# A fused attention, mixture and gated feed-forward kernel: splits, sums and changeover operands moved to neighbouring units, first-layer weights loaded mid-products, the last attention block's normalisation issued first

## The chip, the cores and the metric

The kernel runs on one core of one Trainium2 chip. The metric is the device time of one execution in microseconds (us); the median of three executions of the kernel before is 633.32 us, from 632.99 to 634.52. A measurement of this kernel tells a difference of about 0.3% from none.

The engines are TensorE (PE; PEld is its weight load), VectorE (DVE), ScalarE (ACT), GpSimd (POOL) and SyncE (SP), which issues all transfers.

## The reference, cut to what matters

Three parts run one after the other. All inputs and the output are float32; w_in and w_out reach the chip as 64-bit words.

```python
# q, k, v: (2, 8, 576, 64); a window of 64 keys
scores = q @ k.T / 8, masked to 0 <= row - col < 64
x = softmax(scores) @ v                       # as (1152, 512)

# moe: 4 experts, w1 (4, 512, 1024), w2 (4, 1024, 512)
p = domain_probs / domain_probs.sum(-1)
x = sum over e of p[:, e] * (relu(x @ w1[e]) @ w2[e])

# moe2: w_in (512, 2048), w_out (2048, 512), alpha (2048)
h = x @ w_in
out = (max(h, 0) + alpha * min(h, 0)) @ w_out
```

## The kernel before, in words

Every operand of a product is split into a high and a low part (ACT rounds the high part, `split` at L215, and VectorE or GpSimd subtracts it, `low` at L211), and each product is three matmuls: low by high, high by low, high by high. In names, `wfh`/`wfl` are the first-layer weights, `w2h`/`w2l` the second-layer ones, `xah`/`xal` and `xth`/`xtl` the x operands, `hh`/`hl` the hidden layer.

The 1152 tokens are two halves, p = 0 with 512 and p = 1 with 640. The hidden columns are twelve stages s of 512: stages 0 to 7 are the four experts (two stages each), 8 to 11 (`S1` = 8, `NST` = 12) the second layer pair. Stage 0 runs in chunks of tokens beside the attention (units `LC` and `BC`, four chunks). From stage 1 on a stage is:

- `A` units, seven for each half: the first layer's 2 x 2 block product done as seven products (`PRODUCTS`, L414) with sums of blocks as operands, for two column halves u. Three PSUM banks X, Z and W of each u take several products in turn. `product` (L418) issues the matmuls, copies a bank away on ACT (`keep`, L435), adds it back on VectorE (`total`, L440) and hands the finished quarter to `evict` (L472). A later product adds on to a bank only when the copy or the total has read it.
- `B` units, one for each 128 tokens (four for p = 0, five for p = 1): the second layer (`l2_unit`, L549), 12 matmuls of 512 columns each, added to `acc` by VectorE (ACT in stage 8).

In stages 8 to 11 `evict` only makes r on ACT; `activate` (L518) makes the gated value on VectorE (a head), then its high part on ACT and its low part on GpSimd (a tail); its second argument says how many tails are left waiting. Stage 8 has the order A of half 0, B of half 0 (tokens 2, 3, 0, 1), A of half 1, B of half 1, because its x is the output of stage 7: `x2_unit` (L575) transposes it on TensorE, seven times within stage 7's end and twice within stage 8's first products.

The engines are in order, and the order is written by hand. The list `order` (L682 to L689) holds the units. Every other step hangs on a unit through `plan` (L695): it is issued right behind that unit's own instructions. So hang the sums of first-layer weight blocks (`w_sums`, L174, four GpSimd operations into one buffer `sr` that the next sums can take when its split is done), the splits of first-layer weights (`w_split`, L189) and second-layer weights (`split_w2`, L232), and at the changeover the x operands (`x_first`, `x_sum`, `x_split`, list `changes` at L726). The subtraction on VectorE that ends a split is held until the next unit (`pending`, `settle` at L205).

Weight tiles (`ws`, two buffers of 1 MB) are loaded when the tile two before was last used (`loads`, L768 to L771); SP issues them in the same order of units. The 64-bit words of w_in and w_out are turned to float32 on the chip (`conv_steps`, L251) in steps of three phases, a word tile each three steps: ACT reads the words (L279, L280) and GpSimd ends the tile before (L292, L293); VectorE (L282, L283) and a store; VectorE (L286) and the load of the tile after next. `pace` (L779) says how many of these steps a unit takes.

The attention goes in 18 blocks j of 64 tokens with steps S (scores), E (exponentials), N (normalise: two small VectorE operations, one GpSimd multiply, L330), PT (transposes), PV (product with v) and, five times, X (an x operand of half 0: `x_second`, L395). L605 to L634 write their order; a chunk's units take a share of the list by count, behind each unit.

Of the kernel before, what the change touches and what calls it, by code (L numbers as in the profile page):

```python
# [26 lines left out]
def tile_kernel(ctx, tc, q, k, v, probs, w1, w2, w_in, w_out, alpha, out):  # L27
    nc = tc.nc


    B, H, D, S = k.shape
# [11 lines left out]
    NBLK = B * NB  # L43
    S1 = E * F // FS
    SPE = F // FS
    NST = S1 + F2 // FS
# [19 lines left out]
    def psum(name):  # L66
        return pp.tile([P, 512], F32, tag="ps", name=name)
# [27 lines left out]
    for c in range(1, NCH):  # L95
        n = CHUNK[c + 1] - CHUNK[c]
# [68 lines left out]
    A11, A12, A22, SA1, SA2, SA3, SA4 = range(7)  # L165
# [252 lines left out]
    def product(s, p, u, i):  # L418
        n = HALF[p]
        st = sets.setdefault((s, p, u), {})  # L420
        wi, (kind, f), bank = PRODUCTS[i]
        first = bank not in st
        if first:
            st[bank] = psum(f"{bank}{s}_{p}_{u}")[:, 0:n]
        ps = st[bank]
        wh, wl = [x[:, wi] for x in wf_t[s, u]]
        xh, xl = [x[:, f:f + 2] for x in xa[p]] if kind == "a" else [x[:, f] for x in xt[p]]
        m = 0
        for w, x in ((wl, xh), (wh, xl), (wh, xh)):
            for d in range(2):  # L430
                nc.tensor.matmul(ps, lhsT=w[:, d, :], rhs=x[:, d, :], start=(first and m == 0), stop=(m == 5),  # L431
                                 skip_group_check=True)
                m += 1

        def keep(name):  # L435
            t = late["wfp"].tile([P, HALF[1]], F32, tag=name, bufs=2, name=f"{name}{s}_{p}_{u}")[:, 0:n]
            st[name] = t
            nc.scalar.activation(out=t, in_=ps, func=AF.Copy)  # L438

        def total(name):  # L440
            t = st[name]
            nc.vector.tensor_tensor(out=t, in0=ps, in1=t, op=ALU.add)  # L442
            return t

        if i == 0:
            keep("s1")
        elif i == 1:
            keep("z1")
        elif i == 2:
            keep("u2")  # L450
        elif i == 3:
            evict(s, p, 2 * u, 0, total("s1"))
        elif i == 4:
            evict(s, p, 2 * u + 1, 1, total("z1"))
        elif i == 5:
            evict(s, p, 2 * u, 1, total("u2"))
        else:
            evict(s, p, 2 * u + 1, 0, ps, True)
            del sets[s, p, u]
        if s >= S1:  # L460
            activate(1 if i > 2 else 0, int(i < 5) if s == S1 else (2, 0, 4)[min(i, 2)])
        else:
            low_parts(1)

# [21 lines left out]
    def low_parts(keep):  # L486
        while len(lows) > keep:
            hl, src, hh = lows.pop(0)
            nc.vector.scalar_tensor_tensor(out=hl, in0=src, scalar=0.0, in1=hh.bitcast(F32),
                                           op0=ALU.max, op1=ALU.subtract)  # L490
# [27 lines left out]
    def activate(keep, later):  # L518
        while len(heads) > keep:
            hh, hl, r, col, src, g = heads.pop(0)  # L520
            nc.vector.scalar_tensor_tensor(out=g, in0=r, scalar=col, in1=src, op0=ALU.mult, op1=ALU.add)
            tails.append((hh, hl, g))
        while len(tails) > later:
            hh, hl, g = tails.pop(0)
            nc.scalar.activation(out=hh, in_=g, func=AF.Copy)  # L525
            nc.gpsimd.tensor_tensor(out=hl, in0=g, in1=hh.bitcast(F32), op=ALU.subtract)  # L526
# [54 lines left out]
    with tc.manual_schedule():  # L581
# [22 lines left out]
        steps = []  # L604
        for j in range(NBLK + 4):  # L605
            last = (j - 3) * BLK in CHUNK[1:]
            pv = [("PV", j - 4)] if 0 <= j - 4 < NBLK else []

            if last:
                steps += pv  # L610
            apart = 6 <= j - 1 < 14
            if apart:
                steps.append(("E", j - 1))
            if 0 <= j - 3 < NBLK:
                steps.append(("PT", j - 3))
            if 3 < j <= NBLK and not apart:
                steps.append(("N", j - 1))
            if j < NBLK:
                steps.append(("S", j))
                if not 6 <= j < 14:  # L620
                    steps.append(("E", j))
            if 0 < j <= 3:
                steps.append(("N", j - 1))
            if not last:
                steps += pv
            if apart:
                steps.append(("N", j - 1))
            if 2 <= j < 2 + NF:
                steps.append(("W", j - 2))
            if j % GB == 0 and 3 <= j // GB + 2 < NG:  # L630
                steps.append(("Q", j // GB + 2))

            if 13 <= j < 18:
                steps.append(("X", j - 13))  # L634
        pos = [0]

        def att_step():
# [52 lines left out]
        at = {u: n for n, u in enumerate(order)}  # L690
# [4 lines left out]
        def plan(unit, fn, tid, *args):  # L695
            work.setdefault(at[unit], []).append((fn, tid, args))
# [3 lines left out]
        for s in range(1, NST):  # L700
            if s == 1:
                lc, b = [[(k, NCH - 1, t) for t in range(3)] for k in ("LC", "BC")]
                for u in range(2):
                    plan(lc[u], w_sums, (1, s), s, u, nc.gpsimd)
                for u, part, unit in ((0, A11, ("X1",)), (1, A11, b[0]), (0, SA1, b[0]), (1, SA1, b[1]),
                                      (0, A22, b[2]), (1, A22, b[2])):
                    plan(unit, w_split, (1, s), s, u, part)
            else:
                b = [("B", s - 1, x, t) for x in range(2) for t in range(NTT[x])]
                if s == S1 + 1:  # L710
                    b = [("B", S1, 1, t) for t in (3, 3, 4, 4, 0, 1)]
                plan(("A", s - 1, 1, 0 if s > S1 else 2), w_sums, (1, s), s, 0, nc.gpsimd)
                plan(b[2], w_sums, (1, s), s, 1, nc.gpsimd)
                for n, part in ((0, A11), (0, A22), (1, SA1)):
                    plan(b[n], w_split, (1, s), s, 0, part)
                for n, part in ((2, A11), (3, A22), (4, SA1)):
                    plan(b[n], w_split, (1, s), s, 1, part)
            units = [(0, 1), (0, 2), (1, 0), (1, 1)]
            if s in (1, S1):
                units = [(int(s == 1), i) for i in (0, 0, 1, 1)]  # L720
            for f, (p, i) in enumerate(units):
                plan(("A", s, p, i), split_w2, (2, s), s, f)

        half = {p: [(0, HALF[p] // 2), (HALF[p] // 2, HALF[p] // 2)] for p in range(2)}
        first, second = half[0]
        changes = [(("B", S1 - 1, 0, 3), 0, (0,), (), first), (("B", S1 - 1, 1, 0), 0, (0,), (), second),  # L726
                   (("B", S1 - 1, 1, 0), 0, (), (1, 2, 3, 4), first), (("B", S1 - 1, 1, 1), 0, (), (1, 2, 3, 4), second),
                   (("B", S1 - 1, 1, 1), 0, (1, 2), (), first), (("B", S1 - 1, 1, 2), 0, (1, 2), (), second),
                   (("B", S1 - 1, 1, 2), 0, (3, 5), (), first), (("B", S1 - 1, 1, 3), 0, (3, 5), (), second),
                   (("B", S1 - 1, 1, 4), 0, (4,), (), first), (("B", S1 - 1, 1, 4), 0, (4,), (), second)]  # L730
        for o in half[1]:
            changes += [(("A", S1, 0, 2), 1, (), (1,), o), (("A", S1, 0, 3), 1, (), (2,), o),
                        (("B", S1, 0, 2), 1, (0, 1), (), o), (("B", S1, 0, 3), 1, (2,), (3,), o),
                        (("B", S1, 0, 0), 1, (3, 5), (4,), o), (("B", S1, 0, 1), 1, (4,), (), o)]
        for unit, p, splits, sums, (o, w) in changes:
            for f in splits:
                if f == 0:
# [22 lines left out]
        uses = {}  # L760
# [4 lines left out]
        tids = sorted(uses, key=lambda x: uses[x][0])  # L765
        tids = [(1, 0)] + tids
        uses[1, 0] = [-1]
        loads = {}  # L768
        for n, tid in enumerate(tids):
            if n >= 2:  # L770
                loads.setdefault(uses[tids[n - 2]][-1] + (tids[n - 2][1] > 0), []).append(tid)  # L771

        marks = [steps.index(("PV", CHUNK[c + 1] // BLK - 1)) + 1 for c in range(NCH)]
        per = [len(LC(c) + BC(c)) for c in range(NCH)]
# [3 lines left out]
            load_w(tid)  # L778
        def pace(op, s=0, p=0, i=0):  # L779
            if op == "A":  # L780
                return int(2 <= s < S1 and i < 2 + (s == S1 - 1) or S1 < s < NST - 1 and i in (1, 2))
            if op != "B" or s in (S1 - 1, NST - 2, NST - 1) or (s, p) == (S1, 0):
                return 0
            return 1

        pend = []
        for i, unit in enumerate(order):
            op = unit[0]
# [35 lines left out]
            for _ in range(pace(*unit)):  # L824
                next(late["steps"], None)
# [4 lines left out]
            if op in ("LC", "BC") and unit[1] < NCH - 1:  # L830
                c = unit[1]
                n = (unit[2] if op == "LC" else NF + unit[2]) + 1
# [41 lines left out]
```

## Time and profile before

| | |
|---|---|
| runs of before, median (lowest to highest) | 633.32 us (632.99 to 634.52) |
| the profiled execution's own time | 634.3 us |
| its span, first to last instruction | 632.5 us |
| busy share of the span: TensorE, weight load | 97%, 87% |
| busy share: VectorE, ScalarE, GpSimd | 73%, 50%, 45% |
| mean granted TensorE clock | 0.992 |
| chain that ended last, TensorE's share | 83% |

Times in rows are microseconds from the start of the span, then the duration; `x2` after an operation counts instructions merged into one row. In brackets stands the idle time of the engine before the row and what released it. PEclk is the TensorE clock granted, 1.00 being the full 2.4 GHz and 0.50 the level of 1.2 GHz. A matmul row's duration is longer than its share of the pipeline, so the distance of two starts tells more.

### The profile page before, as it was taken

The numbers are of one execution on the slowest core, as the hardware profiler recorded it, in microseconds if no ns is written. First come the engines' busy times: TensorE is split into PE (matmuls) and PEld (weight loads), VectorE is DVE, ScalarE is ACT, GpSimd is POOL, SyncE is SP. The second block draws the span as 40 slices with busy tenths as digits, with TensorE's granted clock in tenths as the row PEclk, the third lists the DMA queues.
The fourth block names the chain that finished last, engine by engine and source line by source line (L and its number), as shares of the span: only waits on it lengthen the run. The fifth ranks groups of instructions, "written<-read, shape, count | busy, mean of one in ns | idle before, by whom it ended". The sixth has DMA issues, their size and how long they took to land.

```text
span 632.5 us, 10897 instructions
## 1 busy us (share of the span) xinstructions
PE 612.8 (97%) x4032; PEld 548.9 (87%) x4032; DVE 462.6 (73%) x933; ACT 315.7 (50%) x789; POOL 285.4 (45%) x301
## 2 busy tenths in 40 slices
PE   4899999999999999999999999999999999999998
PEld 3688789989989988989989988989788978988986
DVE  3766649778789788788789788757867789763642
ACT  5756526633724624624724624636766662751730
POOL 5645651143443466053443463614735676661440
PEclk8899989999999999999999999999999999999999
DMA  9842001415316225324316224012302124110012
GB/s 323 310 153 68 2 1 64 138 33 183 118 46 205 84 84 183 100 68 167 118 54 196 84 83 150 18 35 98 135 1 108 59 103 136 34 63 1 2 50 101
DMA packets 31653, 62.60 MB, mean 99 GB/s; under 512 B 2288, under 2 KB 11760, under 8 KB 30576
## 3 DMA queue, kind: packets, MB, share of 16 engines
q1 hardware_dynamic: 31600, 61.90, 29.0%
q8 instruction: 32, 0.52, 0.3%
q14 instruction: 21, 0.17, 0.1%
HBM read 51.14 MB, written 10.75 MB: 98 GB/s over the span
## 4 chain that ended last, share of the span: by engine, by line
PE 83%; DVE 5%; ACT 4%; DMA 2%; POOL 2%; issue 2%; SPq 0%; ACTq 0%; POOLq 0%; DVEq 0%
PE o L545 40%; PE X L431 19%; PE Z L431 9%; PE W L431 4%; PE oc L533 4%; PE h L500 3%; ACT p L327 1%; DMA ws<-in_moe_w_dram 1%; PE pv L357 1%; DMA wd<-in_moe_w_in_dram 1%; POOL hl L526 1%; PE s L309 1%; DVE w2l L212 1%; PE pt L340 1%; ACT w2h L219 1%
## 5 line engine op out<-in xcount | busy, mean ns | idle before, releaser
L545 PE MATMUL o<-w2h,hl 128*128 128x512 f32 (+1 forms) x400 | 155.7, 389 | 0.6 <-POOL hl L526 0.5
L545 PE MATMUL o<-w2l,hh 128*128 128x512 f32 (+1 forms) x400 | 155.6, 389 | 0.4 <-ACT hh L525 0.4
L545 PE MATMUL o<-w2h,hh 128*128 128x512 f32 (+1 forms) x400 | 154.9, 387 | 0.0
L292 POOL TENSOR_TENSOR ct<-ct 128x512 f32<-128x512 f32 x32 | 42.7, 1335 | 133.3 <-DVE ct L291 58.1
L545 PEld LDWEIGHTS o<-w2h,hl 128*128 128x128 f32 x400 | 75.1, 188 | 18.3 <-POOL hl L526 3.2
L545 PEld LDWEIGHTS o<-w2l,hh 128*128 128x128 f32 x400 | 75.2, 188 | 15.0 <-ACT hh L525 0.6
L545 PEld LDWEIGHTS o<-w2h,hh 128*128 128x128 f32 x400 | 75.2, 188 | 14.9
L564 DVE SCALAR_TENSOR_TENSOR acc<-o,pn,acc 128x512 f32<-128x512 f32 x63 | 47.1, 748 | 40.7 <-PE o L545 40.6
L187 POOL TENSOR_TENSOR sr<-ws 128x256 f32<-128x256 f32 x44 | 41.6, 944 | 58.9 <-DVE wfl L212 53.0
L212 DVE SCALAR_TENSOR_TENSOR w2l<-ws,w2h 128x512 fp32r<-128x512 f32 x48 | 43.8, 918 | 25.6 <-ACT w2h L219 25.2
L431 PE MATMUL X<-xth,wfl 128*128 128x256 f32 (+1 forms) x264 | 57.4, 298 | 2.8 <-DVE z L442 1.7
L431 PE MATMUL X<-xtl,wfh 128*128 128x256 f32 (+1 forms) x264 | 56.6, 296 | 0.0
L431 PE MATMUL X<-xth,wfh 128*128 128x256 f32 (+1 forms) x264 | 56.6, 296 | 0.0
L293 POOL TENSOR_TENSOR ct<-ct 128x512 f32<-128x512 f32 x32 | 48.3, 1508 | 2.5
L280 ACT ACTIVATE ct<-wd 128x512 f32<-128x512 f32 x32 | 21.3, 665 | 50.8 <-DVE ct L286 50.8
L219 ACT ACTIVATE wfh<-sr 128x1024 fp32r<-128x1024 f32 x22 | 23.1, 1056 | 45.8 <-POOL sr L187 45.8
L431 PEld LDWEIGHTS X<-xth,wfl 128*128 128x128 f32 x264 | 42.5, 190 | 3.8 <-DVE z L442 2.3
L431 PEld LDWEIGHTS X<-xth,wfh 128*128 128x128 f32 x264 | 42.7, 190 | 0.0
L431 PEld LDWEIGHTS X<-xtl,wfh 128*128 128x128 f32 x264 | 42.6, 190 | 0.0
L568 DVE TENSOR_TENSOR acc<-o,acc 128x512 f32<-128x512 f32 (+1 forms) x28 | 18.7, 668 | 29.7 <-PE o L545 29.7
L526 POOL TENSOR_TENSOR hl<-s,hh 128x256 fp32r<-128x256 f32 (+1 forms) x16 | 13.4, 860 | 56.7 <-ACT hh L525 56.7
L438 ACT ACTIVATE s<-X 128x256 f32<-128x256 f32 (+1 forms) x44 | 18.0, 411 | 40.1 <-PE X L431 40.0
(157 smaller groups left out, 1440.5 us busy)
## 6 DMA issues: line engine op xcount, KB each, us to landing
ws<-in_moe_w_dram SPq DMA_DIRECT2D x16, 1024.0 KB, 5.9
wd<-in_moe_w_in_dram SPq DMA_DIRECT2D x16, 512.0 KB, 3.8
cv<-ct SPq DMA_DIRECT2D x32, 256.0 KB, 3.0
wd<-in_moe_w_out_dram SPq DMA_DIRECT2D x16, 512.0 KB, 3.7
ws<-cv SPq DMA_DIRECT2D x8, 1024.0 KB, 5.2
v<-in_v_dram SPq DMA_DIRECT2D x16, 256.0 KB, 5.4
q<-in_q_dram SPq DMA_DIRECT2D x6, 384.0 KB, 6.7
out_dram<-acc SPq DMA_DIRECT2D x8, 256.0 KB, 2.0
```

Of the source, the lines that this page charges most:

```text
L187: e.tensor_tensor(out=t4[:, o], in0=x, in1=y, op=op)
L212: nc.vector.scalar_tensor_tensor(out=lv, in0=src, scalar=1.0, in1=hv.bitcast(F32), op0=ALU.mult, op1=ALU.subtract)
L219: nc.scalar.activation(out=hv, in_=src, func=AF.Copy)
L280: nc.scalar.activation(out=a, in_=top.bitcast(F32), func=AF.Abs, scale=LIFT)
L292: nc.gpsimd.tensor_tensor(out=y, in0=y, in1=e, op=ALU.mult)
L293: nc.gpsimd.tensor_tensor(out=y, in0=r, in1=y, op=ALU.add)
L431: nc.tensor.matmul(ps, lhsT=w[:, d, :], rhs=x[:, d, :], start=(first and m == 0), stop=(m == 5), skip_group_check=True)
L500: nc.tensor.matmul(ps, lhsT=w[:, d * P:(d + 1) * P], rhs=x[:, d, :], start=(m == 0), stop=(m == 3 * KD - 1))
L526: nc.gpsimd.tensor_tensor(out=hl, in0=g, in1=hh.bitcast(F32), op=ALU.subtract)
L533: nc.tensor.matmul(ps, lhsT=h_c[c, f][a][:, t * P:(t + 1) * P], rhs=w_t[2, 0, f][b], start=(n == 0), stop=(n == 3 * NF - 1))
L545: nc.tensor.matmul(ps, lhsT=h_t[s, p, f][a][:, t * P:(t + 1) * P], rhs=w_t[2, s, f][b][:, cols], start=(n == 0), stop=(n == 3 * NF - 1))
L564: nc.vector.scalar_tensor_tensor(out=at, in0=ps, scalar=sc, in1=at, op0=ALU.mult, op1=ALU.add)
```

## The change

In order of the diff: in stage 8 no tail is left waiting. In the attention the normalisation of the last block (j = 17) goes ahead of the transposes of block 15, and each X step is issued one block earlier. For stages 10 and 11 the sums of first-layer weights move from the A units of the stage before into its B units (u = 0 from the first product of half 1 to B unit 1, u = 1 from B unit 2 to B unit 4), and the splits of these sums two units later. Second-layer weights are split at the products 0 and 1 of half 0 in place of 1 and 2. For stage 8's half 1 the first two differences of x move from the A units (GpSimd) to B unit 2 (VectorE), and the splits and sums behind them one unit later each. First-layer weights of stage 2 and later are loaded not before product 3 of half 0 of the stage before. The conversion steps move: stage 7's third step of each half goes, stage 1's B units 1 and 3 take two, stages 9 and 10 take them at the products 0 and 1, and B unit 0 of half 0 takes none from stage 9 on. The name `late_sums` is not used.

```diff
--- before.py
+++ after.py
@@ -458,7 +458,7 @@
             evict(s, p, 2 * u + 1, 0, ps, True)
             del sets[s, p, u]
         if s >= S1:
-            activate(1 if i > 2 else 0, int(i < 5) if s == S1 else (2, 0, 4)[min(i, 2)])
+            activate(1 if i > 2 else 0, 0 if s == S1 else (2, 0, 4)[min(i, 2)])
         else:
             low_parts(1)
 
@@ -611,9 +611,11 @@
             apart = 6 <= j - 1 < 14
             if apart:
                 steps.append(("E", j - 1))
+            if j == NBLK:
+                steps.append(("N", j - 1))
             if 0 <= j - 3 < NBLK:
                 steps.append(("PT", j - 3))
-            if 3 < j <= NBLK and not apart:
+            if 3 < j < NBLK and not apart:
                 steps.append(("N", j - 1))
             if j < NBLK:
                 steps.append(("S", j))
@@ -630,8 +632,8 @@
             if j % GB == 0 and 3 <= j // GB + 2 < NG:
                 steps.append(("Q", j // GB + 2))
 
-            if 13 <= j < 18:
-                steps.append(("X", j - 13))
+            if 12 <= j < 17:
+                steps.append(("X", j - 12))
         pos = [0]
 
         def att_step():
@@ -709,13 +711,15 @@
                 b = [("B", s - 1, x, t) for x in range(2) for t in range(NTT[x])]
                 if s == S1 + 1:
                     b = [("B", S1, 1, t) for t in (3, 3, 4, 4, 0, 1)]
-                plan(("A", s - 1, 1, 0 if s > S1 else 2), w_sums, (1, s), s, 0, nc.gpsimd)
-                plan(b[2], w_sums, (1, s), s, 1, nc.gpsimd)
-                for n, part in ((0, A11), (0, A22), (1, SA1)):
+                late_sums = s > S1 + 1
+                behind = 2 * (s > S1 + 1)
+                plan(b[1] if behind else ("A", s - 1, 1, 0 if s > S1 else 2), w_sums, (1, s), s, 0, nc.gpsimd)
+                for n, part in ((0, A11), (0, A22), (1 + behind, SA1)):
                     plan(b[n], w_split, (1, s), s, 0, part)
-                for n, part in ((2, A11), (3, A22), (4, SA1)):
+                plan(b[2 + behind], w_sums, (1, s), s, 1, nc.gpsimd)
+                for n, part in ((2, A11), (3, A22), (4 + behind, SA1)):
                     plan(b[n], w_split, (1, s), s, 1, part)
-            units = [(0, 1), (0, 2), (1, 0), (1, 1)]
+            units = [(0, 0), (0, 1), (1, 0), (1, 1)]
             if s in (1, S1):
                 units = [(int(s == 1), i) for i in (0, 0, 1, 1)]
             for f, (p, i) in enumerate(units):
@@ -729,9 +733,11 @@
                    (("B", S1 - 1, 1, 2), 0, (3, 5), (), first), (("B", S1 - 1, 1, 3), 0, (3, 5), (), second),
                    (("B", S1 - 1, 1, 4), 0, (4,), (), first), (("B", S1 - 1, 1, 4), 0, (4,), (), second)]
         for o in half[1]:
-            changes += [(("A", S1, 0, 2), 1, (), (1,), o), (("A", S1, 0, 3), 1, (), (2,), o),
-                        (("B", S1, 0, 2), 1, (0, 1), (), o), (("B", S1, 0, 3), 1, (2,), (3,), o),
-                        (("B", S1, 0, 0), 1, (3, 5), (4,), o), (("B", S1, 0, 1), 1, (4,), (), o)]
+            changes += [(("B", S1, 0, 2), 1, (0,), (1,), o), (("B", S1, 0, 3), 1, (1,), (), o),
+                        (("B", S1, 0, 0), 1, (2, 5), (3,), o), (("B", S1, 0, 1), 1, (3,), (), o),
+                        (("A", S1, 1, 0), 1, (4,), (), o)]
+        for unit, f in ((("B", S1, 0, 2), 2), (("B", S1, 0, 1), 4)):
+            changes += [(unit, 1, (), (f,), o) for o in half[1]]
         for unit, p, splits, sums, (o, w) in changes:
             for f in splits:
                 if f == 0:
@@ -768,7 +774,10 @@
         loads = {}
         for n, tid in enumerate(tids):
             if n >= 2:
-                loads.setdefault(uses[tids[n - 2]][-1] + (tids[n - 2][1] > 0), []).append(tid)
+                free = uses[tids[n - 2]][-1] + (tids[n - 2][1] > 0)
+                if tid[0] == 1 and tid[1] > 1:
+                    free = max(free, at["A", tid[1] - 1, 0, 3])
+                loads.setdefault(free, []).append(tid)
 
         marks = [steps.index(("PV", CHUNK[c + 1] // BLK - 1)) + 1 for c in range(NCH)]
         per = [len(LC(c) + BC(c)) for c in range(NCH)]
@@ -778,10 +787,10 @@
             load_w(tid)
         def pace(op, s=0, p=0, i=0):
             if op == "A":
-                return int(2 <= s < S1 and i < 2 + (s == S1 - 1) or S1 < s < NST - 1 and i in (1, 2))
-            if op != "B" or s in (S1 - 1, NST - 2, NST - 1) or (s, p) == (S1, 0):
+                return int(2 <= s < S1 and i < 2 or S1 < s < NST - 1 and i < 2)
+            if op != "B" or s in (S1 - 1, NST - 2, NST - 1) or (s, p) == (S1, 0) or s > S1 and (p, i) == (0, 0):
                 return 0
-            return 1
+            return 1 + (s == 1 and p == 0 and i % 2)
 
         pend = []
         for i, unit in enumerate(order):
```

## Rows read from the trace of the kernel before

**Rows 1.** The page, busy time by engine: us (share of the span) xinstructions.

```profile
PE 612.8 (97%) x4032; PEld 548.9 (87%) x4032; DVE 462.6 (73%) x933; ACT 315.7 (50%) x789; POOL 285.4 (45%) x301
```

**Rows 2.** The chain of waits, TensorE's pieces: start us, us, what.

```profile
196.16 1.43 PE X L431 x12
...
243.06 1.43 PE X L431 x12
...
290.65 1.43 PE X L431 x12
...
416.93 2.78 PE o L545 x12
420.14 2.76 PE o L545 x12
...
436.13 1.44 PE X L431 x12
...
486.64 1.43 PE X L431 x12
...
510.99 24.51 PE o L545 x108
535.50 1.43 PE X L431 x12
```

**Rows 3.** The timeline of TensorE, rows with idle time before them.

```profile
79.51 0.66 PE L340 MATMUL pt<-ident,p 128*128 128x128 f32 x4 [1.79 <-POOL p L334]
...
251.97 0.50 PE L431 MATMUL X<-xth,wfl 128*128 128x256 f32 x2 [0.28 <-DVE z L442]
...
391.31 0.50 PE L431 MATMUL X<-xth,wfl 128*128 128x256 f32 x2 [1.12 <-ACT u L438]
...
448.66 0.50 PE L545 MATMUL o<-w2h,hl 128*128 128x512 f32 x1 [0.46 <-POOL hl L526]
...
495.67 0.50 PE L431 MATMUL X<-xth,wfl 128*128 128x256 f32 x2 [0.40 <-DVE z L442]
...
508.90 0.56 PE L431 MATMUL X<-xth,wfl 128*128 128x320 f32 x2 [0.97 <-DVE z L442]
```

**Rows 4.** Busy us by stretch: PE, PEld, DVE, ACT, POOL, then PEclk, DMA, GB/s.

```profile
80.00:84.00 4.00, 4.00 (x40) 3.41 (x39) 1.87 (x4) 0.38 (x1) 3.76 (x7) 0.57 0.02 4
...
391.00:392.00 1.00, 0.69 (x5) 0.69 (x6) 0.94 (x3) 1.00 (x3) 0.31 (x1) 1.00 0.00 0
```

**Rows 5.** The timeline of GpSimd.

```profile
77.19 1.27 POOL L401 TENSOR_TENSOR xtl<-tr,xth 128x512 fp32r<-128x512 f32 x1
78.42 1.04 POOL L334 TENSOR_TENSOR p<-p,st 128x512 f32<-128x512 f32 x1
...
441.64 2.60 POOL L389 TENSOR_TENSOR tr<-raw,tr 128x320 f32<-128x320 f32 x2
445.98 1.76 POOL L526 TENSOR_TENSOR hl<-s,hh 128x256 fp32r<-128x256 f32 x2 [1.73 <-ACT hh L525]
...
506.22 1.19 POOL L187 TENSOR_TENSOR sr<-ws,sr 128x256 f32<-128x256 f32 x1
...
524.11 1.13 POOL L187 TENSOR_TENSOR sr<-ws 128x256 f32<-128x256 f32 x1 [1.16 <-DVE wfl L212]
```

**Rows 6.** The timeline of VectorE.

```profile
250.35 1.22 DVE L212 SCALAR_TENSOR_TENSOR w2l<-ws,w2h 128x512 fp32r<-128x512 f32 x1
...
441.27 2.23 DVE L212 SCALAR_TENSOR_TENSOR w2l<-ws,w2h 128x512 fp32r<-128x512 f32 x2 [0.52 <-ACT w2h L219]
...
452.73 0.92 DVE L212 SCALAR_TENSOR_TENSOR xal<-raw,xah 128x640 fp32r<-128x640 f32 x1 [2.60 <-ACT xah L219]
...
542.02 0.68 DVE L212 SCALAR_TENSOR_TENSOR w2l<-ws,w2h 128x512 fp32r<-128x512 f32 x1
```

**Rows 7.** The timeline of ScalarE, a conversion step of stage 7.

```profile
389.77 0.67 ACT L279 ACTIVATE ct<-wd 128x512 f32<-128x512 uint32 x1 [1.45 <-DMA wd<-in_moe_w_in_dram]
```

**Rows 8.** The page, transfers: what, queue, count, KB each, median us to landing.

```profile
ws<-in_moe_w_dram SPq DMA_DIRECT2D x16, 1024.0 KB, 5.9
```

## The prediction

> **What bounds the kernel now.** I read the page first, for the engine that is full. TensorE is busy for 612.8 of 632.5 us [rows 1], so at most 19.7 us can come back unless work is taken off TensorE, and the change takes none off: every product stays.
>
> Then I read the chain of waits for where the stages begin. A stage s is seven product steps for each half of the tokens (the A units) and nine output units (the B units). Stage 3 runs from 196.16 to 243.06, which is 46.90 us, and the whole stage is TensorE work [rows 2]. That is the yardstick. Stage 4 takes 47.59, so 0.69 is lost. Stages 5 to 7 together take 145.48, which is 4.78 over three times 46.90. Seven sets of transposes lie in stage 7; each lengthens an output unit from 2.72 (24.51 / 9) to 3.21, 0.49 each, 3.4 in all, and the other 1.4 us are lost. Stage 8 takes 50.51: less 46.90 and two more sets of transposes, 2.6 are lost. Stage 9 takes 48.86, so 1.96 are lost. Together 6.6 us.
>
> Third, TensorE's timeline tells where these losses sit and who released them [rows 3]. The first of them, at 79.51, belongs to the attention: 1.79 us of waiting for GpSimd's multiply of the last block's probabilities. Behind it the granted clock is 0.57 of full speed over the 4 us from 80 to 84 [rows 4], which costs 4 x 0.43 = 1.7 us more. At 251.97, 495.67 and 508.90 the seventh product of a set waits: it adds to the bank X, which VectorE's total behind the fifth has to read first. The wait at 391.31 is the same kind, on ScalarE's copy of the third. The one at 448.66 is an output unit that waits for the low half of its operand from GpSimd.
>
> So there is 1.8 + 1.7 + 0.7 + 1.4 + 2.6 + 2.0 = 10.2 us that a better order could give back, and the start (before 24 us) is not touched.
>
> **The change part by part.**
>
> *Attention.* GpSimd's last multiply (1.04 us) starts at 78.42, right behind the low split of the fifth x operand, 1.27 us from 77.19 [rows 5]. The change issues that x step one block earlier, and VectorE's two small operations for the multiply ahead of its copy of the transposes of block 15. The multiply so comes at least 78.42 - 77.19 = 1.23 us earlier, by the x step alone; with VectorE's part I take 1.5, so 0.3 of the 1.79 stays. The x step itself is only moved: its cost lies beside TensorE's products, whose timeline shows no wait from 24 to 77 us. The clock: behind the hole of 1.12 us at 391.31 the granted clock stayed at 1.00 [rows 3, 4], so I expect no fall behind a hole of 0.3 and take the 1.7 back. Sum 3.2; bounds 0 (the multiply is bound by its exponentials) and 3.5.
>
> The Trainium skill (TensorE: Matmul & The Clock Gate, What's actually happening) says that the clock's observation is free-running, so where it falls differs between runs of one kernel. By that the 1.7 us might be lost in a run after all, and the sum would be 1.5; the rows here, half clock behind 1.79 us and full clock behind 1.12, speak for the length of the hole.
>
> *Second-layer splits one product earlier, conversion steps shifted* (stages 2 to 7, 9 to 11). In stage 4 VectorE does the low split of the second tile at 250.35 for 1.22 us, between the totals [rows 6]; the total of z came behind it and TensorE waited. With the splits at the first two products the low halves are written before the first total exists, so this op leaves the stretch in which the totals are due. I take 0.6 of 0.69 in stage 4. In stage 9 the wait of 0.40 at 495.67 is the same case; there the price is the op itself, 0.68 without GpSimd beside it [rows 6]. ScalarE now has a split ahead of the second copy, 0.6 us in a place where it waited for TensorE: no cost, and if its cover went it would delay the copy by as much.
>
> *Stage 7.* ScalarE stood 1.45 us behind a late load of words to convert [rows 7], and the copy of the third product behind it. The change takes the third conversion step out of stage 7 (two more are done in stage 1, in output units, where a late step delays nothing that TensorE waits for), and the 1 MB weight load no longer runs beside those words. I take 1.3 of 1.4.
>
> *First-layer weights loaded at the fourth product.* The load (5.9 us to landing [rows 8]) stands on SP behind one store and one load of the conversion. From the fourth product of the first half to the third of the second are six products of 1.43 us [rows 2] or more, 8.6 us; its first reader, GpSimd's sums, may come later still, since the splits of these sums are due in the output units. Cost 0; if the cover went, sums and splits would slide and nothing else, up to the point in the rival below. In stage 8 the load for stage 9 now comes behind that of the second layer; its reader is 15 us away.
>
> *Stage 8, the changeover.* Two things kept the low halves late. GpSimd did two differences in 2.60 us from 441.64 beside VectorE's two splits, 2.23 us from 441.27 [rows 5, 6]; alone two such splits take 1.36, so the totals start 0.9 earlier. And each finished head waited for one more before its high and low halves were made; now they follow at once, one product's turn (0.7 us) earlier. GpSimd's chain, which began at 445.98, moves by up to 1.6. The waits of the first output units sum to 2.0 and those of the second half to 0.6; I take 2.2 of 2.6. What is added: four differences on VectorE in the output units. VectorE idles there for 2.60 us [rows 6], and GpSimd's price of 1.30 each bounds them at 5.2; nearer is VectorE's 0.68 for a larger two-operand op, 2 us in all, so they fit. The operand of the seventh product is now split in the first product of the second half, six products ahead of its use: cost 0, bound 1.
>
> *Stage 9 and 10, sums of first-layer weights.* In stage 9 GpSimd's four sums (the last ends at 507.4) stood ahead of the low halves of the first token half and beside VectorE's totals [rows 5], and TensorE waited at 508.90. Moved into the output units they are out of both ways. With the splits I take 1.7 of 1.96.
>
> **Sum.** 3.2 + 0.6 + 1.3 + 2.2 + 1.7 = 9.0. The profiled execution took 634.3 us (632.5 of span and 1.8 around it) and comes to 625.3. It stood 1.0 above the median of the runs, 633.32, so the median to come is 624.3.
>
> **Rivals.**
>
> *The attention's hole stays.* Because five x steps moved, the count of steps per chunk shifts too, and the last exponentials are issued one product group later. If the multiply then waits for them, the 1.79 and the clock remain: 633.3 - 5.8 = 627.5. Against it: the rows show the multiply behind another GpSimd operation, not idle. Chance 0.13.
>
> *The stalls move.* The conversion's three phases fall on other units than before, two steps on; stage 4's pattern now falls on stages 2 and 5. If each lost 0.7 to 1.4 again, and stage 9 one of its two waits, 3 us are given back: 627.3. For it: stages with the same code differ by pattern alone. Against: no total has a split in front of it any more. Chance 0.19.
>
> *Late sums in stages 9 and 10* (slower). The second set of sums needs the buffer that the first set's split frees. Before, it began at 524.11, 13.1 us into the output units (510.99), having waited for VectorE [rows 2, 5]. Two units (5.4 us) later that is 18.5. Four sums at 1.13 follow, 4.5, and a split of 1024 columns on each of two engines, an estimate of 1.3 on ScalarE (twice the 0.67 for 512 [rows 7]) and 1.4 on VectorE (twice 0.68 [rows 6]): the operand stands at 25.7. The product that reads it starts at 24.5 and one and a half products, 26.7. A slip of over 1.0 us decides; from there every microsecond is paid once in each of two stages. To end slower than before it takes 5.7 us in each: 636 with 6.5. The Trainium skill (GPSIMD Engine Reference, Key points) says that GpSimd contends with VectorE operations of two SBUF inputs, which speaks against sums beside splits; the trace agrees, 1.22 against 0.68 us for one split [rows 6], and that is in the 13.1 already. Chance 0.05.
>
> *Nothing to be measured.* The late sums concern only the last two loads and the rest is a reshuffle within each engine's slack; gains in one stage are eaten in another and the sum is under 1.9: 632.5. Chance 0.06.
>
> **How the numbers follow.** The forecast has 0.57: 624.3. A measurement tells about 0.3% here, 1.9 us. Low end: all 10.2 back, 623.1, less 0.5 for the spread of the runs. High end: both middle rivals, each at its worst, 629. That leaves out the last two rivals (0.11) and some of the spread. Faster 0.88, within 0.3% 0.07, slower 0.05.
>
> **What would show it.** Right: stages 2 to 6, 9 and 10 each 46.9 us long; no TensorE wait above 0.4 us after 100 us; the multiply of block 17 before 77.5 us with the clock at 1.00 from 80 to 84; stage 8 under 48.4. Wrong: a wait of TensorE on VectorE's first-layer split at the start of stage 10 or 11 (late sums); on ScalarE's copies in stages 2 or 5 (moved stalls); the hole at 79 us still there.

## The result, and the profile after

The kernel after takes 625.98 us (median of four runs, 625.48 to 626.92), the kernel before, beside it, 633.58: a ratio of 0.988, 95% interval 0.9863 to 0.9898. The profiled execution is the slowest of the four, 626.92 us with 624.9 of span. Forecast were 624.3 us and a range of 622.6 to 629.0.

The page, busy time by engine, and its line on the chain that ended last (against [rows 1]):

```profile
PE 610.9 (98%) x4032; PEld 549.2 (88%) x4032; DVE 468.9 (75%) x937; ACT 316.6 (51%) x789; POOL 280.7 (45%) x297
...
PE 96%; DMA 1%; ACT 1%; DVE 1%; SPq 0%; issue 0%
```

Before, TensorE held 83% of the chain. Now almost nothing else is on it. The chain, TensorE's first product of stages 1 to 4, 5, 7 and 8 to 11 (against [rows 2]; start us, us, what):

```profile
100.86 1.43 PE X L431 x12
...
147.85 1.43 PE X L431 x12
...
194.75 1.43 PE X L431 x12
...
241.65 1.43 PE X L431 x12
...
288.55 1.43 PE X L431 x12
...
382.35 1.43 PE X L431 x12
...
432.56 1.44 PE X L431 x12
...
480.99 1.43 PE X L431 x12
...
527.89 1.43 PE X L431 x12
...
574.79 1.43 PE X L431 x12
```

Subtract neighbours. Stages 2, 3, 4, 9 and 10 are 46.90 us each (stage 1 46.99). Stage 7 is 50.21, its seven transposes included, so 1.47 came back: stages 5 to 7 took 145.48 before and take 2 x 46.90 + 50.21 = 144.01. Stage 8 is 48.43 in place of 50.51. Stage 4 gained 0.69, stage 9 1.96. Stage 1 begins at 100.86 in place of 102.26, so all ahead of it gained 1.40. The sum is 1.40 + 0.69 + 1.47 + 2.08 + 1.96 = 7.6, the difference of the spans.

TensorE's timeline has no idle row behind 81 us. The last one, and GpSimd's chain ahead of it (against [rows 3, 5]; start, duration, idle before and releaser):

```profile
80.66 0.69 PE L357 MATMUL pv<-ptr,v 128*64 128x64 f32 x16 [0.17 <-DVE ptr L344]
```

```profile
74.36 1.28 POOL L401 TENSOR_TENSOR xtl<-tr,xth 128x512 fp32r<-128x512 f32 x1
75.60 1.04 POOL L334 TENSOR_TENSOR p<-p,st 128x512 f32<-128x512 f32 x1
...
77.75 1.05 POOL L334 TENSOR_TENSOR p<-p,st 128x512 f32<-128x512 f32 x1
```

The hole of 1.79 at 79.51 is gone. Why the start then gained 1.40 and not 3, the granted clock tells (PE, PEld, DVE, ACT, POOL busy, then PEclk, DMA, GB/s; the first two lines are of before, the others of after):

```profile
22.00:24.00 2.00, 1.77 (x20) 1.65 (x20) 1.97 (x10) 0.78 (x4) 1.59 (x2) 0.50 1.07 388
24.00:26.00 2.00, 2.00 (x23) 1.34 (x22) 1.52 (x8) 1.80 (x9) 1.85 (x4) 0.64 0.94 296
```

```profile
22.00:24.00 2.00, 1.65 (x19) 1.53 (x20) 1.97 (x10) 0.78 (x3) 1.59 (x2) 0.50 1.05 387
24.00:26.00 2.00, 2.00 (x21) 1.34 (x20) 1.51 (x10) 1.93 (x9) 1.85 (x4) 0.50 1.01 308
26.00:28.00 2.00, 2.00 (x11) 2.00 (x11) 0.93 (x10) 0.00 (x0) 1.20 (x2) 0.50 0.98 348
28.00:30.00 2.00, 2.00 (x17) 2.00 (x16) 1.00 (x5) 0.90 (x2) 0.14 (x1) 0.85 0.54 186
...
80.00:84.00 4.00, 3.83 (x44) 3.14 (x42) 1.72 (x4) 0.39 (x1) 3.76 (x7) 1.00 0.01 4
```

From 80 to 84 the clock is 1.00 (before, 0.57 [rows 4]). But from 22 to 30 us, where both kernels issue the same instructions, it stays at 0.50 for longer: the loss is 2 x (0.50 + 0.50 + 0.50 + 0.15) = 3.3 us, against 2 x (0.50 + 0.36) = 1.7 in the profile of before (0.50, 0.64, then 1.00). The second layer's products of the third chunk so start 1.57 us later than before (TensorE's timeline, before and then after), the first layer's of the fourth chunk 1.39 earlier (84.33 against 85.72 in the chain):

```profile
73.65 0.50 PE L533 MATMUL oc<-w2l,hch 128*128 128x512 f32 x1
```

```profile
75.22 0.50 PE L533 MATMUL oc<-w2l,hch 128*128 128x512 f32 x1
```

The attention's own gain is 2.96, and 1.57 was lost to the clock long ahead of it.

### The profile page after: what moved, and what is told of

Read it like the earlier page. It is cut to its first block, busy times and chain, and to the rows that moved or that the text cites. A ratio compares the mean times of both kernels' runs of the same rounds, so it can differ in the third digit from the quotient of the medians.

```text
span 624.9 us, 10887 instructions
## 1 busy us (share of the span) xinstructions
PE 610.9 (98%) x4032; PEld 549.2 (88%) x4032; DVE 468.9 (75%) x937; ACT 316.6 (51%) x789; POOL 280.7 (45%) x297
## 4 chain that ended last, share of the span: by engine, by line
PE 96%; DMA 1%; ACT 1%; DVE 1%; SPq 0%; issue 0%
PE o L545 43%; PE X L431 23%; PE Z L431 11%; PE W L431 6%; PE h L500 5%; PE oc L533 4%; PE pv L357 1%; DMA ws<-in_moe_w_dram 1%; PE pt L340 1%; PE s L309 1%; ACT p L327 1%; PE x L578 1%; ACT w1h L228 0%; ACT ptr L346 0%; SPq L117 0%
## 5 line engine op out<-in xcount | busy, mean ns | idle before, releaser
L293 POOL TENSOR_TENSOR ct<-ct 128x512 f32<-128x512 f32 x32 | 47.3, 1478 | 2.5
L431 PE MATMUL Z<-xth,wfl 128*128 128x320 f32 (+1 forms) x176 | 37.9, 296 | 0.0
```

The lines of the kernel that those rows point to most:

```text
L293: nc.gpsimd.tensor_tensor(out=y, in0=r, in1=y, op=ALU.add)
```

## The experiments

My theory: each part gives back its own stage's loss, and the 1.5 us between the terms' sum and the profile is the clock near 25 us, which varies by execution. Rivals: the parts need each other; the longer half clock is the change's own doing. Eight of the kernels below ran once each: `x_only`, and seven at 626.20 to 629.71 us. The times of the seven aren't compared, since the clock near 25 us moves an execution by as much as a part does; the lengths of their stages are, because from stage 2 to 6 a stage without a stall is 46.9 us to within 0.04 in every profile.

**The attention.** Three kernels. `att_only` is the kernel before with these lines, `x_only` with the last four of them alone, `att_undone` the kernel after without them.

```diff
+            if j == NBLK:
+                steps.append(("N", j - 1))
...
-            if 3 < j <= NBLK and not apart:
+            if 3 < j < NBLK and not apart:
...
-            if 13 <= j < 18:
-                steps.append(("X", j - 13))
+            if 12 <= j < 17:
+                steps.append(("X", j - 12))
```

> The kernel before with the attention's two moves alone (block 17's normalisation ahead of block 15's transposes, each X step one block earlier). My theory, each part gives back its own loss: TensorE's wait of 1.79 us at 79.5 and the half clock from 80 to 84 are gone, stage 1 begins about 3.0 us earlier for the same clock before 45 us, stages 4, 7, 8 and 9 keep their 47.6, 51.7, 50.5 and 48.9 us; the time is 3.0 us under before, 630.5. Rival, the longer half clock near 25 us is the change's own doing: stage 1 begins only 1.4 us earlier and the stretch of half clock behind the hole at 22.3 lasts to 29 us in this kernel too, in every run: 632. Rival, it is the run's: that stretch is long in some runs and short in others, in kernels with and without these moves.

> The kernel after with the attention as before. My theory: the hole of 1.8 us at 79.5 comes back with the half clock behind it, stages 1 to 11 stay at 46.9 but for 50.2 in stage 7 and 48.4 in stage 8; 3.0 us slower than after, 6.2 faster than before: 627.3. Rival, the parts help each other (late work from the attention feeds the losses of stages 4 to 9): those stages lose again and the time is above 629.

> The kernel before with only the X steps one block earlier. If GpSimd's low split ahead of the multiply was what made it late, the multiply of block 17 starts 1.2 us or more before 78.42 and of the hole of 1.79 at most 0.6 is left, with the clock at 1.00 from 80 to 84: about 630.5 to 631.5. If it was VectorE's two small operations, queued behind its copy of the transposes of block 15 and behind exponentials, the multiply starts within 0.3 us of 78.42 and the hole and the half clock stay: about 633.

`att_only` took 632.01 us beside 634.52 for before, 0.996 (0.9944 to 0.9976); `att_undone` 628.59 on the same chip, 0.9909 (0.9883 to 0.9935); `x_only` 631.79 in its one execution. The moves alone are worth 2.5 us, the rest alone 5.9, together 8.4; the change's own ratio makes 7.6, which lies within these intervals. In `att_only` stages 4, 7, 8 and 9 keep their losses, and in `att_undone` stages 1 to 11 are as in after while this row is back, with a granted clock of 0.59 from 80 to 84:

```profile
80.14 0.66 PE L340 MATMUL pt<-ident,p 128*128 128x128 f32 x4 [1.75 <-POOL p L334]
```

So this part stands by itself. `x_only` has all of it (GpSimd's timeline, then its first product of stage 1):

```profile
76.37 1.04 POOL L334 TENSOR_TENSOR p<-p,st 128x512 f32<-128x512 f32 x1
```

```profile
99.48 1.43 PE X L431 x12
```

The multiply starts 2.05 us earlier than 78.42, and stage 1 2.78 earlier than in before. In `att_only` it starts at 76.76 and stage 1 at 99.87, both 0.4 later than in `x_only`: in these executions the moved normalisation adds nothing.

**Stage 7 and the loads.** `pace_undone` puts `pace` back to that of the kernel before, `load_undone` the loads:

```diff
-                if tid[0] == 1 and tid[1] > 1:
-                    free = max(free, at["A", tid[1] - 1, 0, 3])
```

> The kernel after with the conversion's steps as in the kernel before (stage 7 takes its third step of each half again). If the third step was what put ScalarE behind late words, stage 7 is 51.3 to 51.7 us in place of 50.2, with a TensorE wait of about 1.1 on ScalarE's copy. If the weight load beside those words was the cause, which this kernel keeps moved, stage 7 stays at 50.2. In both cases the other stages stay at 46.9 and 48.4, unless the steps at the second and third product of stages 9 and 10 cost something: then stage 9 is 47.0 to 47.3.

> The kernel after with first-layer weights loaded as early as in the kernel before. If the load beside the words made them late, stage 7 is 51.0 us or more in place of 50.2 and ScalarE waits for words; if the third step did, stage 7 stays at 50.2 and nothing else changes. My own forecast: 50.2, the load alone costs nothing once the third step is gone. Stages 2 to 6 stay at 46.9 by both.

`pace_undone`: stage 7 is 51.11 us, 0.90 more, TensorE waiting for VectorE's total of z and not for ScalarE's copy as expected; 0.4 are lost in stages 9 and 10.

```profile
390.26 0.51 PE L431 MATMUL X<-xth,wfl 128*128 128x256 f32 x2 [0.65 <-DVE z L442]
```

So the third step was the larger part of stage 7's 1.47. Whose the other 0.57 is stays open: the load undone alone costs stage 7 nothing, and no kernel has both undone. `load_undone`: stage 7 stays at 50.21, as forecast, but what I had ruled out came: stages 1 and 2 together lose 1.4 us and stages 4 and 5 together 0.5 (their lengths from the chain, 95.30 and 94.28, against 93.89 and 93.80). SyncE's queue, ScalarE's and TensorE's timelines of this kernel:

```profile
145.13 0.39 SPq L144 DMA_DIRECT2D ws<-in_moe_w_dram  x1
146.74 0.34 SPq L155 DMA_DIRECT2D wd<-in_moe_w_out_dram  x1
```

```profile
152.84 0.67 ACT L279 ACTIVATE ct<-wd 128x512 f32<-128x512 uint32 x1 [1.49 <-DMA wd<-in_moe_w_out_dram]
```

```profile
154.39 0.50 PE L431 MATMUL X<-xth,wfl 128*128 128x256 f32 x2 [1.17 <-ACT u L438]
...
295.58 0.50 PE L431 MATMUL X<-xth,wfl 128*128 128x256 f32 x2 [0.24 <-ACT u L438]
```

The 1 MB load stands 1.6 us ahead of the words, the words land 6 us after their issue, ScalarE stands behind them, and the copy of the third product behind ScalarE: [rows 7] over again, in stages 2 and 5. In after the words that ScalarE reads at 151.62, without a wait, were issued at 147.14, and the load comes only at 152.45.

**Stage 8.** `tails_undone` leaves one tail waiting, `xdiff_undone` has the first x differences of half 1 on GpSimd again:

```diff
-            activate(1 if i > 2 else 0, 0 if s == S1 else (2, 0, 4)[min(i, 2)])
+            activate(1 if i > 2 else 0, int(i < 5) if s == S1 else (2, 0, 4)[min(i, 2)])
```

```diff
+            changes += [(("A", S1, 0, 2), 1, (), (1,), o), (("A", S1, 0, 3), 1, (), (2,), o),
...
-        for unit, f in ((("B", S1, 0, 2), 2), (("B", S1, 0, 1), 4)):
-            changes += [(unit, 1, (), (f,), o) for o in half[1]]
```

> The kernel after with one tail left waiting in stage 8 up to the fifth product. My theory: every low half comes one product's turn later, GpSimd's chain starts 0.7 later than 8.3 us into the stage, and of the 2.1 us that stage 8 gave back 0.7 is lost again: stage 8 is 49.1 us. Rival, the chain is held up by VectorE's totals whatever the tails: 48.4, unchanged. All other stages as in after.

> The kernel after with half 1's x differences of the changeover as in the kernel before (the first two in stage 8's product steps on GpSimd). My theory: VectorE's two pairs of low splits take 1.5 and 2.2 us again beside them in place of 1.3 each, the totals start 0.9 later, and stage 8 is 49.3 us in place of 48.4. Rival, the differences hold GpSimd itself, so its chain starts later still: 49.7 or more. Rival, the tails alone made the gain: 48.4. All other stages as in after.

Stage 8 is 49.80 us (+1.37) in the first and 50.35 (+1.92) in the second, all others as in after. Each cost more than I expected, and together 3.3, more than the 2.08 gained: with either one back, most of the gain is gone. GpSimd in `xdiff_undone`, where stage 8 begins at 432.95:

```profile
441.49 0.80 POOL L526 TENSOR_TENSOR hl<-s,hh 128x256 fp32r<-128x256 f32 x1 [2.99 <-ACT hh L525]
442.25 2.08 POOL L389 TENSOR_TENSOR tr<-raw,tr 128x320 f32<-128x320 f32 x2
444.30 0.90 POOL L526 TENSOR_TENSOR hl<-s,hh 128x256 fp32r<-128x256 f32 x1
```

The rival that the differences hold GpSimd itself is right: two of them sit between the first two low halves, for 2.08 us, and an output unit waits 1.75 for the halves behind. In after the chain of low halves begins 8.28 us into the stage and runs without a break (first row GpSimd, second VectorE, which has the differences now):

```profile
440.84 1.69 POOL L526 TENSOR_TENSOR hl<-s,hh 128x256 fp32r<-128x256 f32 x2 [12.13 <-ACT hh L525]
```

```profile
445.74 1.44 DVE L389 TENSOR_TENSOR tr<-raw 128x320 f32<-128x320 f32 x2
```

In `tails_undone` that chain begins 8.91 us into the stage, 0.63 later, and the weight load of the output units waits for it eight times, 3.2 us in all, against four times and 1.2 in after: each unit pays for the lateness again until GpSimd has caught up.

**Second-layer splits.** `splits_undone` has the two products back at 1 and 2.

```diff
-            units = [(0, 0), (0, 1), (1, 0), (1, 1)]
+            units = [(0, 1), (0, 2), (1, 0), (1, 1)]
```

> The kernel after with the second-layer splits at the products 1 and 2 again. My theory: the low split between the totals is what stage 4 and one wait of stage 9 lost, so stage 4 is 47.4 to 47.6 us and stage 9 is 47.3 or more; other stages may lose 0.2 to 0.7 where a conversion step falls on the same product. Rival, the conversion's steps and the moved loads are enough without it: all stages stay at 46.9.

Stages 4 and 9 stay at 46.9. Stage 2 takes 47.47 and stage 10 47.54. VectorE, then TensorE:

```profile
155.03 1.78 DVE L212 SCALAR_TENSOR_TENSOR w2l<-ws,w2h 128x512 fp32r<-128x512 f32 x1
```

```profile
157.21 0.50 PE L431 MATMUL X<-xth,wfl 128*128 128x256 f32 x2 [0.32 <-DVE z L442]
...
537.87 0.50 PE L431 MATMUL X<-xth,wfl 128*128 128x256 f32 x2 [0.37 <-DVE z L442]
```

The mechanism is that of stage 4 before (a low split ahead of the total of z, 1.78 us here against 1.22 in [rows 6]), but it has moved, two stages on, with the conversion's phases. With the splits moved, in after, no stage from 2 to 7 and neither 9 nor 10 has it.

**The sums of first-layer weights.** `sums_undone` has the two `w_sums` back in the product steps; `sums_later` reads

```diff
-                behind = 2 * (s > S1 + 1)
+                behind = 4 * (s > S1 + 1)
```

> The kernel after with the sums of first-layer weights for stages 10 and 11 back in the product steps of the stage before, as in the kernel before. My theory: the wait of 0.97 us of stage 9's last product comes back, stage 9 is 47.9 us, and stage 10, which had no wait in the kernel before either, stays at 46.9. Rival, the splits at the first two products took that wait away with the other: both stages stay at 46.9. Rival, each of the two is enough for one part only: stage 9 is between 47.2 and 47.6.

> The kernel after with the sums of stages 10 and 11 two output units later still (the second set in unit 2 of half 1, its split in unit 4). In after the split of the second set ends at 527.87 and its first reader, the second column half of the second product, starts at 529.88, so 2.0 us are to spare. Two units are 5.4 us: TensorE waits 3.4 us for VectorE's split in the second product of stage 10, and the same in stage 11, about 6.8 us in all over after. By the prediction's own margin of 1.0 us it would be 4.4 in each, 8.8 in all. Rival, GpSimd and VectorE are freer in the later units and the split comes sooner: under 2 us in each.

`sums_undone`: stage 9 is 47.66 us, 0.76 more, with a wait for VectorE's total of z at the seventh product, where before had 0.97; stage 10 stays.

```profile
501.55 0.56 PE L431 MATMUL X<-xth,wfl 128*128 128x320 f32 x2 [0.51 <-DVE z L442]
```

That lies between my 47.9 and the last rival's 47.6, nearer the rival: splits and sums shared that loss. `sums_later` loses 3.87 us, all in stage 10 (TensorE's timeline, then the windows):

```profile
531.08 0.80 PE L431 MATMUL Z<-xth,wfl 128*128 128x256 f32 x2 [2.14 <-DVE wfl L212]
```

```profile
530.00:532.00 2.00, 0.92 (x4) 0.92 (x5) 2.00 (x3) 0.00 (x0) 0.00 (x0) 0.76 0.34 131
532.00:534.00 2.00, 2.00 (x11) 2.00 (x11) 0.80 (x3) 0.90 (x2) 1.28 (x1) 0.50 0.03 8
534.00:536.00 2.00, 2.00 (x17) 2.00 (x16) 0.81 (x2) 0.77 (x2) 1.62 (x1) 0.89 0.00 0
```

The operand is written 4.4 us into the stage in place of 0.14 (527.87 in after). It came 4.25 later, not 5.4, above all because the split took 1.21 us there and not 2.06; less 2.0 to spare that leaves 2.25, and 2.14 were waited. The clock then fell: 2 x (0.24 + 0.50 + 0.11) = 1.7 us, which no expectation had. In stage 11, whose first product starts at 577.40, the operand is ready at 579.43 and its reader starts at 579.54: no wait, by 0.11 us. In stage 10 VectorE has two operations of the conversion right ahead of the split (L282 and L283, from 527.44 to 529.81), in stage 11 none.

**A better order near 20 us.** Both kernels keep the whole change. `start_early` takes block 3's copy off ScalarE, lets the fourth first-layer split and block 5's normalisation come behind block 6's exponentials, and splits block 2's x on ScalarE and VectorE; `start_order` issues scores ahead of the normalisation in blocks 4 to 6 too, and two splits one block later.

```diff
-        if j % 2 and j >= NF:
+        if j % 2 and j >= NF - 1:
...
-        if (j + 1) * BLK in CHUNK:
+        if (j + 1) * BLK in CHUNK or j == 2:
...
+            if j == 7:
+                steps.append(("N", 5))
...
-            if 3 < j < NBLK and not apart:
+            if 6 < j < NBLK and not apart:
...
-            if 0 < j <= 3:
+            if 0 < j <= 5:
...
-            if 2 <= j < 2 + NF:
-                steps.append(("W", j - 2))
+            if j in (2, 4, 5, 7):
+                steps.append(("W", (2, 4, 5, 7).index(j)))
...
-        while pos[0] < marks[0] + 4:
+        while pos[0] < marks[0] + 6:
```

That is `start_order`; `start_early` has `3 < j < NBLK and j != 6`, `0 < j <= 3` and splits at j = 2, 3, 4 and 7.

> The kernel after with another order near 20 us: the copy of block 3's transposes on VectorE, the fourth first-layer split and block 5's normalisation behind block 6's exponentials, and block 2's x split on ScalarE and VectorE. My theory: the hole of 2.03 us at 22.3 is ScalarE's queue (four exponentials and a split ahead of that copy), and the half clock behind it comes from the hole. Then no TensorE wait above 1.2 us stands between 19 and 25 us, the first product of the first layer begins at about 23 in place of 25.5, and with the clock at 1.00 from 22 to 30 us stage 1 begins 3 to 5 us earlier than in after: 621 to 623. Rival, the half clock there is a matter of the first 30 us whatever the order: only the 2 us of waiting come back, 624. Rival, the waits move to the next block's normalisation: no gain, 626.

> The kernel with the earlier order near 20 us, and in blocks 4 to 6 the scores' row minimum ahead of the last block's normalisation on VectorE, which waits for exponentials; the second first-layer split one block later, the third one too. My theory: what is left between 17 and 22 us (waits of 0.5, 0.5 and 1.15 us) is VectorE's order, block j's scores behind the normalisation of block j-1; with the order turned the first product of the first layer starts at 21.5 to 22.5 in place of 23.2 and the time is 1 to 2 us under the 624 of the earlier order. Rival, ScalarE's exponentials are full there and set the pace: 23.2 again, the same time.

`start_early` takes 624.06 us beside 634.52 for before, 0.9839 (0.981 to 0.9868). Its timeline and windows:

```profile
21.43 0.69 PE L357 MATMUL pv<-ptr,v 128*64 128x64 f32 x16 [1.15 <-DVE ptr L344]
...
23.23 0.74 PE L500 MATMUL h<-xah,w1l 128*128 128x256 f32 x4
```

```profile
22.00:24.00 2.00, 2.00 (x30) 1.62 (x27) 1.97 (x12) 1.84 (x10) 1.04 (x3) 1.00 1.06 386
24.00:26.00 2.00, 2.00 (x19) 2.00 (x18) 1.97 (x12) 1.87 (x5) 1.62 (x2) 1.00 0.86 297
```

In after that row reads

```profile
22.35 1.12 PE L357 MATMUL pv<-ptr,v 128*64 128x64 f32 x16 [2.03 <-ACT ptr L346]
```

The hole of 2.03 us is 1.15, the clock stays at 1.00 in this profile, the first product comes at 23.23 in place of 25.52, and stage 1 begins 3.66 us earlier than in after, at 97.20. The order's own part is nearer 2.2: `sums_undone`, whose clock is 1.00 from 22 to 32 us too, begins stage 1 at 99.38. `start_order` takes 622.98 beside 634.56, 0.9826 (0.98 to 0.9851), an interval below the change's own and the lowest median here; from `start_early` the intervals don't part it. Of its expected 1 to 2 us it gave 0.65 (stage 1 begins at 96.55, the first product at 22.56), since the wait for block 3's copy stayed:

```profile
20.76 0.69 PE L357 MATMUL pv<-ptr,v 128*64 128x64 f32 x16 [1.49 <-DVE ptr L344]
```

That copy now stands behind VectorE's low split of a first-layer weight. The theory holds in part; ScalarE waits for VectorE ahead of block 5's exponentials (0.67 at 18.91), so it isn't full.

**The clock near 25 us.** Twelve profiles, all but those two kernels', are of the same instructions up to about 45 us. From 22 to 32 us the windows give 1.7 us lost in six of them (before, `att_only`, `att_undone`, `x_only`, `load_undone`, `sums_later`), 3.2 to 3.4 in four (after, `tails_undone`, `xdiff_undone`, `splits_undone`) and none in two, `pace_undone` and `sums_undone`. The latter:

```profile
22.31 0.69 PE L357 MATMUL pv<-ptr,v 128*64 128x64 f32 x16 [1.81 <-ACT ptr L346]
```

```profile
22.00:24.00 2.00, 1.69 (x36) 1.39 (x36) 1.97 (x10) 1.04 (x4) 1.59 (x2) 1.00 1.05 386
24.00:26.00 2.00, 1.05 (x13) 0.67 (x6) 2.00 (x14) 1.73 (x9) 1.85 (x4) 1.00 1.03 315
```

So the long stretch in after is no doing of any one part: kernels with the attention's moves have all three cases. One execution of each can't show how often each comes. Nor did the two kernels keep the clock: their half clock stands earlier, behind a hole of 2.1 us that ends near 11 us and that all profiles have. `sums_undone` again:

```profile
12.00:14.00 2.00, 1.75 (x17) 1.42 (x20) 1.19 (x10) 1.71 (x7) 1.06 (x2) 0.50 1.05 387
14.00:16.00 2.00, 2.00 (x28) 1.51 (x24) 0.37 (x1) 2.00 (x8) 1.40 (x2) 0.50 1.06 394
16.00:18.00 2.00, 2.00 (x27) 1.34 (x27) 1.79 (x12) 1.19 (x7) 1.15 (x2) 0.50 1.06 381
```

From 12 to 20 us that is 3.3 us by the windows, and it costs the start nothing: the first layer's first product comes at 25.05, against 25.40 in before, since TensorE waits at 22.31 for ScalarE's copy all the same. What differs between executions is where the half clock falls, and so whether it costs time.

## Why the prediction was right, and where it was not

**The sum.** 9.0 was forecast; the terms measured 2.96 + 0.69 + 1.47 + 2.08 + 1.96 = 9.16 (3.2, 0.6, 1.3, 2.2 and 1.7 forecast). The step that failed is the one that set this sum against the execution's own time: it took the start before 24 us as untouched and so as equal. The profile of after lost 1.6 us more to the half clock at 22 to 30 us, so the two profiles are 7.6 apart. That the medians are 7.6 apart too isn't shown to have this cause: no traces of the other executions are kept, and their mean granted clock doesn't order their times (before, beside `att_only`: 633.10 to 633.68 us at 1.000, 633.60 to 634.52 at 0.992, 635.16 to 636.14 at 0.995). The terms came out near because each loss was read off the chain of before and almost all came back; that doesn't vouch for the causes given for them.

**Attention.** Right in place and nearly in size. The two parts were not: the x step moved the multiply by 2.05 and not by 1.23, VectorE's operations by nothing. The rival that the hole stays fell; the last exponentials, which it feared late, start at 73.27 in `x_only` against 72.88, and that cost nothing. The sign of being right, the multiply before 77.5, was missed at 77.75, in a profile that was 1.57 late by then.

**The clock.** I argued that the length of the hole decides (1.79 against 1.12). Behind 1.75 in `att_undone` and 1.68 in `load_undone` it fell, behind 1.81 in `sums_undone` and 1.50 in `pace_undone` it did not: length alone doesn't decide. The Trainium skill (TensorE: Matmul & The Clock Gate, What's actually happening) says that the observation is free-running and that the cold stretch varies between runs of one kernel; the trace agrees, with 0, 1.7 or 3.3 us lost from 22 to 32 us in one and the same piece of code. From 80 to 84 us the clock is 1.00 in all twelve profiles with the x steps moved, 0.57 and 0.59 in the two without: the 1.7 came back in these profiles, but that it is always lost behind the hole isn't shown.

**Stages 4, 7 and 9.** Sizes right, owners wrong. I gave stage 4 to the splits: with them undone, stages 2 and 10 lose. I costed the load's move at nothing and credited it inside stage 7: undone, stage 7 loses nothing and stages 1 to 5 lose 1.9. The rival that the stalls move, to stages 2 and 5, had the mechanism; the moved load and the moved splits are what kept it from happening.

**Stage 8.** 2.08 against 2.2, at 48.43 just short of the sign, under 48.4. I had the differences slow VectorE's splits (they do, 1.55 us a pair in place of 1.3); the larger harm was that they would stand in GpSimd's chain.

**Late sums.** No wait at the start of stages 10 and 11, as forecast. The margin is 2.0 us, twice the 1.0 worked out. That a slip is paid in each of two stages is wrong: in `sums_later` only the stage behind the conversion pays, and then with a fall of the clock on top.

## What to carry to other kernels

Where a periodic helper (here the conversion) walks through the stages, don't cure the stage that shows the stall: undo one part of the cure at a time and see where the stall goes. Price a hole of two microseconds on TensorE at up to twice its length, since the clock may fall behind it (2.14 cost 3.87 here; behind 1.81 it did not fall). And set a sum of terms against a median only after looking at what the clock did in the stretches that the change doesn't touch.

## What had not been expected of the hardware

The same first 45 us lost 1.7 us to the granted clock in two profiles, 3.4 in nine and 5.1 in one, at different places. The records of the clock don't show all of it: in after the 4 transposes at 10.65 and the 16 score products at 11.70 take 1.11 and 1.13 us, against 0.66 and 0.67 at 15.85 and 16.44, while the windows there say 1.00.

One two-operand split of 128x512 on VectorE took 0.68 us in `sums_later` at 531.55 and 1.78 in `splits_undone` at 155.03, where GpSimd adds words beside it (L293, 1.50 us from 154.77); in `sums_later` GpSimd is idle until 532.71.
